# Float64 weights to two float32 words: low words added to 16 bits of the pattern in one operation, and two batches of k-v products moved to a later block

## The chip, the cores and the metric

The kernel runs on one core of a Trainium2 chip. The metric is the device time of one execution in microseconds, and the value before is the median of three runs. A profile is one further execution, taken by the hardware profiler.

## The reference, cut to what matters

```python
kv = np.einsum('bhsd,bhse->bhde', k, v)                # 8 batches, 8 heads, 576 tokens, 64 wide
out = np.einsum('bhsd,bhde->bhse', q, kv)
out = out / sqrt(mean(out * out, -1) + 1e-06) * g_norm
x = out as 4608 tokens x 512
h = x @ w_in                                           # w_in 512 x 2048, float64
x = (maximum(h, 0) ** 2) @ w_out                       # w_out 2048 x 512, float64
e = argmax(x @ w_gate + modality_bias[modality_id])    # 8 experts
out = softmax weight of e * (maximum(x @ w1[e], 0) @ w2[e])
```

w_in and w_out are float64 in memory. All products are made in float32 on TensorE, and each weight is split into a high and a low part of TensorE's own float32 format, so that one product of the reference is three products of the kernel (high by high, high by low, low by high).

## The kernel before, in words

The attention and the dense layer are one loop (phase 1) over 12 blocks of 2 to 4 token tiles of 128 tokens. A block j runs 16 iterations i. In each, `emit_h` makes one 128-wide slice of x @ w_in (12 matmuls into the tile `hps`), ScalarE and VectorE make the squared relu and split it (`relu`, `square`, `rest`, tile `ghl`), and `emit_x` adds the slice of two iterations earlier times w_out into the tiles `acc` (3 matmuls for each token tile). The attention of the next block's tiles runs between: `q_load`, `att_one`, `att_norm`, `att_tr`. Later blocks also compute the gate and split the expert weights w1 and w2 (`u_load`, `u_split`, `u_store`). After the 12 blocks follow the expert slots (phase 2).

Block 0 is different: it also turns the float64 weights into float32 parts. The weights are 32 pieces of 512 KB (16 of w_in, 16 of w_out, in the order in which they are used), and a piece is loaded raw into one of NRAW = 4 places of the tile `wq` (`w_load`). Every float64 is there as two 32-bit words, `low` and `up`. Iteration i of block 0 handles two pieces at each step: `w_sum`, `w_part` on pieces 2i + 4 and 2i + 5, `w_scale` and `w_join` on the next two. The steps are:

- `w_scale` (ScalarE): multiplies `up`, read as float32, by a power of two into the tile `conv` (L303). For three pieces of four it also turns `up` into a bare sign bit (L307, L308).
- `w_join` (VectorE): shifts the scaled pattern by three bits and sets the sign (L317 for two pieces at once, or L324, or L328 and L329 where the sign was not prepared).
- `w_sum` (VectorE): takes sign and exponent of the pattern (L339), multiplies the low word by it (L340), and adds that to the pattern as float32 (L342). As soon as L340 has read the low word, the place in `wq` is free and `w_load` of the piece four later is issued on the SP queue.
- `w_part`: ScalarE copies the high part (L356), and the low part is the difference (L354), on VectorE for w_in and on GpSimd (POOL) for w_out.

The order of every engine is the order in which the code is written; nothing reorders it. The SP queue issues nearly all loads in that order too, so a load that waits for its buffer holds up every load behind it.

The k-v products of a batch (`kv_load`, `kv_mm`) need 4 loads of 480 KB and 2 of 192 KB, and 4 groups of 20 small matmuls (tile `kvps`). Batch 0 comes ahead of block 0. Batches 1, 2 and 3 (FIRST = 4) are made in block 0, one group or two per iteration, into the tiles `early`. The products of batches 2 and 3 are stored in DRAM (`kvd`, L177) and fetched back by `kv_get` in a later block, because only two product tiles (`kvbd`) are kept. Batches 4 to 7 are made in blocks 5, 6, 8 and 9, two groups at iteration 2 and two at iteration 4, with loads into tiles of the pool `t4`.

Ahead of block 0 the SP queue loads weight pieces 0 to 3 between the k-v parts of batch 0 and the first four q tiles. VectorE converts four pieces before it turns to the sums of squares of the first tiles.

Of the kernel before, what the change touches and what calls it, by code (L numbers as in the profile page):

```python
# [10 lines left out]
F32 = mybir.dt.float32  # L11
# [3 lines left out]
U32 = mybir.dt.uint32  # L15
AF = mybir.ActivationFunctionType
# [23 lines left out]
NKV = 2  # L40

FIRST = 4
NRAW = 4
# [3 lines left out]
def body(ctx: ExitStack, tc: tile.TileContext, qT, kvp, kvr, g_norm, w_in, w_out, mod, wg, wgd, mb, w1, w2, out):  # L47
# [12 lines left out]
    kvd = dram.tile([FIRST, 128, 4, 64], F32, name="kvd")  # L60
# [68 lines left out]
    def kv_load(b, hp):  # L129
# [27 lines left out]
    def kv_mm(b, hp):  # L157
# [8 lines left out]
        if hp == 3:  # L166
            kvps.pop(b)
            if b < NKV or b >= FIRST:
                t = kvbd[b % NKV]
                lo, up = t[0:64, :, 0:64], t[64:128, :, 64:128]  # L170
            else:
                t = one.tile([128, 4, 64], F32, tag="x", name="kvs")
                lo, up = t[0:64], t[64:128]
            nc.scalar.activation(out=lo, in_=ps[0:64, :, 0:64], func=AF.Copy)
            nc.scalar.activation(out=up, in_=ps[64:128, :, 64:128], func=AF.Copy)
# [3 lines left out]
    def kv_get(b):
        t = kvbd[b % NKV]  # L180
        for h in range(2):
            c = slice(64 * h, 64 * h + 64)
            nc.sync.dma_start(out=t[c, :, c], in_=kvd[b, c])
# [106 lines left out]
    xb = p1b.tile([128, 512], U32, tag="sq", name="xb")  # L290
# [21 lines left out]
    def w_join(n, c=2):  # L312
        if n < NP:
            low, up, a = w_at(n, c)

            if n % 4 == 0 and c == 2:
# [3 lines left out]
                return  # L320
            for m in range(c):
                am, um = a[:, m], up[:, m]
                if (n + m) % 4 < 3:
                    nc.vector.scalar_tensor_tensor(  # L324
                        out=am, in0=am, scalar=3, in1=um, op0=ALU.logical_shift_left, op1=ALU.bitwise_or
                    )
                else:
                    nc.vector.tensor_scalar(out=am, in0=am, scalar1=3, scalar2=None, op0=ALU.logical_shift_left)  # L328
                    nc.vector.scalar_tensor_tensor(  # L329
# [846 lines left out]
```

## Time and profile before

| What | us |
|---|---|
| Median of three runs | 1466.36 (1461.36, 1466.36, 1468.72) |
| The profiled execution's own time | 1462.47 |
| Its span in the trace | 1460.7 |
| PE busy | 1405.7 (96%) |
| DVE busy | 794.5 (54%) |
| ACT busy | 534.9 (37%) |
| POOL busy | 451.3 (31%) |
| Chain that ended last | PE 81%, DVE 8%, DMA 4%, ACT 3% |

PE is TensorE, DVE VectorE, ACT ScalarE, POOL GpSimd, and SPq the queue of SyncE that issues loads. The busy shares are means over very different stages, and a busy PE is not PE at its peak, since its matmuls overlap. The trace can be cut into stretches: the preparation before the first matmul of block 0 (to 36.77 us), block 0 (to 162.78 us, where block 1's first matmul starts), the other blocks, and the expert slots from about 943 us on.

### The profile page before, as it was taken

How to read it: one execution, taken by the hardware profiler on the slowest of the kernel's cores; microseconds unless marked ns; L12 is line 12 of the kernel's file. 1: busy time of each engine (PE TensorE's matmuls, PEld its weight loads, DVE VectorE, ACT ScalarE, POOL GpSimd, SP SyncE). 2: the span in 40 equal slices, each digit the busy share in tenths (PEclk: the TensorE clock that was granted, in tenths of full speed). 3: DMA queues.
4: the chain of work that ended last, by engine and by line, in shares of the span. 5: the costliest groups of instructions: out<-in, count | busy, mean ns of one | idle time of the engine just before them, and what ended most of it. 6: DMA issues, size and time to landing. Idle time of an engine off the chain costs nothing.

```text
span 1460.7 us, 24807 instructions
## 1 busy us (share of the span) xinstructions
PE 1405.7 (96%) x7682; PEld 1211.8 (83%) x7682; DVE 794.5 (54%) x1618; ACT 534.9 (37%) x965; POOL 451.3 (31%) x392
## 2 busy tenths in 40 slices
PE   5698999999999999999999999999999999999997
PEld 4577798988998888988888988888888888888886
DVE  5798577868785658685858677262222222222221
ACT  5687434444333334433434433332222222222221
POOL 1123223635324434443434441222222222222210
PEclk9899999999999999999999999999999999999999
DMA  7974225665536565666566640644114623357762
GB/s 209 222 215 149 98 73 192 197 201 199 167 105 199 177 191 184 213 192 187 194 173 205 209 169 23 261 151 159 44 45 154 214 101 102 121 205 263 266 254 87
DMA packets 80817, 247.33 MB, mean 169 GB/s; under 512 B 15790, under 2 KB 16046, under 8 KB 72368
## 3 DMA queue, kind: packets, MB, share of 16 engines
q1 hardware_dynamic: 69552, 208.83, 44.1%
q0 software_dynamic: 8832, 20.09, 4.3%
q10 hardware_dynamic: 2304, 16.78, 2.9%
q8 instruction: 70, 1.15, 0.3%
q14 instruction: 59, 0.48, 0.1%
HBM read 414.59 MB, written 87.96 MB: 344 GB/s over the span
## 4 chain that ended last, share of the span: by engine, by line
PE 81%; DVE 8%; DMA 4%; ACT 3%; issue 2%; POOL 1%; SPq 0%; DVEq 0%; POOLq 0%; ACTq 0%
PE hps L395 22%; PE hps L901 15%; PE yps L938 15%; PE acc L445 7%; PE acc L443 7%; PE acc L444 7%; PE htp L926 2%; DMA wq<-w_in 2%; DVE ghl L430 1%; PE ops L211 1%; DVE r L429 1%; PE xps L881 1%; PE tps L267 1%; DVE xb L340 1%; DMA wq<-w_out 1%
## 5 line engine op out<-in xcount | busy, mean ns | idle before, releaser
L395 PE MATMUL hps<-xt,wa 128*128 128x384 f32 (+2 forms) x2304 | 441.0, 340 | 1.1 <-ACT xt L270 0.8
L395 PEld LDWEIGHTS hps<-xt,wa 128*128 128x128 f32 x2304 | 403.5, 189 | 24.3 <-ACT xt L270 1.2
L379 POOL TENSOR_TENSOR hl<-raw,hl 128x512 fp32r<-128x512 f32 x128 | 178.7, 1403 | 256.1 <-ACT hl L378 255.7
L938 PE MATMUL yps<-wb,hq 128*128 (+1 forms) x960 | 234.2, 399 | 0.4 <-ACT hq L927 0.4
L901 PE MATMUL hps<-wa,xq 128*128 (+1 forms) x960 | 233.7, 399 | 0.0
L443 PE MATMUL acc<-wb,ghl 128*128 128x512 f32 x576 | 231.0, 401 | 0.0
L445 PE MATMUL acc<-wb,ghl 128*128 128x512 f32 x576 | 227.4, 395 | 3.5 <-DVE ghl L430 3.5
L444 PE MATMUL acc<-wb,ghl 128*128 128x512 f32 x576 | 226.1, 393 | 0.0
L467 DVE SCALAR_TENSOR_TENSOR junk<-x,wg_sb 128x512 f32<-128x512 f32 x264 | 218.3, 827 | 4.8
L938 PEld LDWEIGHTS yps<-wb,hq 128*128 128x128 f32 x960 | 177.5, 188 | 41.2 <-ACT hq L927 0.7
L901 PEld LDWEIGHTS hps<-wa,xq 128*128 128x128 f32 x960 | 177.3, 188 | 39.6
L429 DVE TENSOR_TENSOR r<-r 128x384 f32<-128x384 f32 (+1 forms) x160 | 108.9, 681 | 177.4 <-ACT ghl L422 177.0
L412 ACT ACTIVATE r<-hps 128x384 f32<-128x384 f32 (+2 forms) x192 | 93.7, 488 | 295.8 <-PE hps L395 291.0
L430 DVE TENSOR_TENSOR ghl<-r,ghl 128x384 fp32r<-128x384 f32 (+2 forms) x192 | 138.5, 722 | 51.3 <-ACT r L424 33.1
L928 DVE TENSOR_TENSOR hq<-htp,hq 128x512 fp32r<-128x512 f32 x80 | 51.5, 686 | 206.2 <-ACT hq L927 206.2
L945 POOL DMA_INDIRECT out<-y,me x40 | 40.7, 1018 | 351.4 <-ACT y L944 287.5
L378 ACT ACTIVATE hl<-raw 128x512 fp32r<-128x512 f32 x128 | 80.2, 626 | 144.7 <-DMA raw<-w 101.3
L445 PEld LDWEIGHTS acc<-wb,ghl 128*128 128x128 f32 x576 | 108.0, 188 | 28.6 <-DVE ghl L430 4.8
L443 PEld LDWEIGHTS acc<-wb,ghl 128*128 128x128 f32 x576 | 108.4, 188 | 18.0 <-issue 0.5
L444 PEld LDWEIGHTS acc<-wb,ghl 128*128 128x128 f32 x576 | 108.4, 188 | 17.9
L422 ACT ACTIVATE ghl<-r 128x384 fp32r<-128x384 f32 (+2 forms) x192 | 100.9, 526 | 6.0
L944 ACT ACTIVATE y<-yps,me 128x512 f32<-128x512 f32 x40 | 27.5, 687 | 203.1 <-PE yps L938 192.3
(157 smaller groups left out, 1147.4 us busy)
## 6 DMA issues: line engine op xcount, KB each, us to landing
wa<-wd SPq DMA_DIRECT2D x148, 1024.0 KB
wb<-wd SPq DMA_DIRECT2D x144, 1024.0 KB
wd<-hl SPq DMA_DIRECT2D x128, 512.0 KB
raw<-w SPq DMA_DIRECT2D x128, 256.0 KB
x2buf<-x SPq DMA_DIRECT2D x36, 256.0 KB
wq<-w_in SPq DMA_DIRECT2D x16, 512.0 KB
wq<-w_out SPq DMA_DIRECT2D x16, 512.0 KB
qt<-qt SPq DMA_DIRECT2D x32, 256.0 KB
```

What stands on the lines that cost most here:

```text
L379: nc.gpsimd.tensor_tensor(out=hl[:, 1, :].bitcast(F32R), in0=t, in1=hl[:, 0, :], op=ALU.subtract)
L395: nc.tensor.matmul(ps[:, 0:128 * BLK[j]], wav[:, i, wi, k, :], xt[:, xi, k, :], start=(n == 0), stop=(n == 11))
L412: nc.scalar.activation(out=rs[i], in_=hps.pop(i)[:, 0:c], func=AF.Relu)
L422: nc.scalar.activation(out=g2[0], in_=r, func=AF.Square)
L429: nc.vector.tensor_tensor(out=r, in0=r, in1=r, op=ALU.mult)
L430: nc.vector.tensor_tensor(out=g2[1], in0=r, in1=g2[0].bitcast(F32), op=ALU.subtract)
L443: nc.tensor.matmul(a, g2[0][:, sl], wbv[:, i, 0, :], start=(i == 0), stop=False)
L444: nc.tensor.matmul(a, g2[0][:, sl], wbv[:, i, 1, :], start=False, stop=False)
L445: nc.tensor.matmul(a, g2[1][:, sl], wbv[:, i, 0, :], start=False, stop=(i == NF - 1))
L467: nc.vector.scalar_tensor_tensor(out=junk, in0=x2s[j, t], scalar=1.0, in1=wg_sb[:, e, :], op0=ALU.mult, op1=ALU.mult, accum_out=lgs[j][:, ...
L901: nc.tensor.matmul(hp[f], xq[:, xi, k, :], rhs(wa, s, o + 512 * wi), start=(k == 0 and n == 0), stop=(k == 3 and n == 2),)
L938: nc.tensor.matmul(ps, hq[:, hi, k, :], rhs(wb, s, 1024 * k + 512 * wi), start=(k == 0 and n == 0), stop=(k == 7 and n == 2),)
```

## The change

The change has four parts.

1. `w_sum` becomes one VectorE operation for two pieces: the low word times 2**-29 is added to the low 16 bits of the joined pattern (a 16-bit view of every second halfword), and the sum is rounded to 16-bit integers. L339, L340, L342 and the tile `xb` go. Both loads of the pieces four later are issued behind that one operation.
2. `w_scale` prepares the sign bit for one piece of four only, and `w_join` therefore uses the two-operation form for three pieces of four. The low parts of w_out are subtracted on VectorE, not on GpSimd.
3. The products of batches 2 and 3 move from block 0 to blocks 1 and 3, in the form that batches 4 to 7 have. The store and fetch through `kvd` go. The q tiles of block 1's attention are loaded at iterations 4, 7 and 10 of block 0, before at 6, 8 and 10. The units of the expert weights have fewer places in blocks 2 and 3, and the last of them move to blocks 10 and 11.
4. Ahead of block 0 the k-v parts of batch 0 are loaded first, then q tiles and weight pieces in turn. Only pieces 0 and 1 are converted before the attention of the first tiles is through; pieces 2 to 5 follow behind it.

```diff
-FIRST = 4
 NRAW = 4
...
-        if b < FIRST:
+        if b < NKV:
             t = early[-1][0:120, n % 3 if b else hp]
...
-            if NKV <= b < FIRST:
-                nc.sync.dma_start(out=kvd[b], in_=t)
...
-            k = sum(m % 4 < 3 for m in range(n, n + c))
-            if k:
-                up = up[:, 0:k]
+            if n % 4 == 0:
+                up = up[:, 0]
...
     def w_join(n, c=2):
+        for n in range(n, min(n + c, NP)):
+            low, up, a = (t[:, 0] for t in w_at(n, 1))
+            if n % 4 == 0:
                 nc.vector.scalar_tensor_tensor(
                     out=a, in0=a, scalar=3, in1=up, op0=ALU.logical_shift_left, op1=ALU.bitwise_or
                 )
+            else:
+                nc.vector.tensor_scalar(out=a, in0=a, scalar1=3, scalar2=None, op0=ALU.logical_shift_left)
+                nc.vector.scalar_tensor_tensor(
+                    out=a, in0=up, scalar=0x80000000, in1=a, op0=ALU.bitwise_and, op1=ALU.bitwise_or
+                )
...
     def w_sum(n, c=2):
-        for n in range(n, min(n + c, NP)):
-            low, up, a = w_at(n, 1)
-            low, a = low[:, 0], a[:, 0]
-            x = xb.bitcast(F32)
-            nc.vector.tensor_scalar(out=xb, in0=a, scalar1=0xFF800000, scalar2=None, op0=ALU.bitwise_and)
-            nc.vector.scalar_tensor_tensor(out=x, in0=low, scalar=2.0**-52, in1=x, op0=ALU.mult, op1=ALU.mult)
-            w_load(n + NRAW)
-            nc.vector.tensor_tensor(out=a.bitcast(F32), in0=a.bitcast(F32), in1=x, op=ALU.add)
+        if n < NP:
+            low, up, a = w_at(n, c)
+            h = a.bitcast(U16).rearrange("p m (f c) -> p m f c", c=2)[:, :, :, 0]
+            nc.vector.scalar_tensor_tensor(out=h, in0=low, scalar=2.0**-29, in1=h, op0=ALU.mult, op1=ALU.add)
+            for m in range(c):
+                w_load(n + m + NRAW)
...
-                eng = nc.gpsimd if m else nc.vector
-                eng.tensor_tensor(out=p[1], in0=w, in1=p[0].bitcast(F32), op=ALU.subtract)
+                nc.vector.tensor_tensor(out=p[1], in0=w, in1=p[0].bitcast(F32), op=ALU.subtract)
...
+    for hp in range(4):
+        kv_load(0, hp)
+    q_load(0)
     w_load(0)
-    kv_load(0, 0)
+    q_load(1)
+    q_load(2)
     w_load(1)
-    kv_load(0, 1)
-    kv_load(0, 2)
+    q_load(3)
     w_load(2)
-    kv_load(0, 3)
-    q_load(0)
-    q_load(1)
     w_load(3)
-    q_load(2)
-    q_load(3)
...
+    w_part(1, True, 1)
+    w_join(2)
+    w_sum(2)
+    w_scale(4)
+    w_part(2, False)
     w_join(4)
+    w_part(2, True)
...
-            if b < FIRST:
-                i = max(n // 2, n - 2)
+            if b < NKV:
+                i = n // 2
...
-                i0 = 2 * n + 6 if j == 0 else 3 * n + 3
+                i0 = 3 * n + (4 if j == 0 else 3)
...
-            for b in kv_gt.get((j, i), []):
-                kv_get(b)
```

How the change moves instructions, at three places. The first is VectorE in the middle of block 0, one iteration of the program before, from one `rest` (L430) to the next. `conv` is the joined pattern, `wq` the raw words, `xb` the factor for the low word.

```order
L430 TENSOR_TENSOR ghl<-r,ghl 128x512
L324 SCALAR_TENSOR_TENSOR conv<-conv,wq 128x512
L328 TENSOR_SCALAR conv<-conv 128x512
L329 SCALAR_TENSOR_TENSOR conv<-wq,conv 128x512
L354 TENSOR_TENSOR wa<-conv,wa 128x512
L339 TENSOR_SCALAR xb<-conv 128x512
L340 SCALAR_TENSOR_TENSOR xb<-wq,xb 128x512
L342 TENSOR_TENSOR conv<-conv,xb 128x512
L339 TENSOR_SCALAR xb<-conv 128x512
L340 SCALAR_TENSOR_TENSOR xb<-wq,xb 128x512
L342 TENSOR_TENSOR conv<-conv,xb 128x512
```

The same iteration on VectorE in the changed program, where L403 is `rest`, L300, L304 and L305 are `w_join`, L327 is the low part and L314 is the new sum.

```order
L403 TENSOR_TENSOR ghl<-r,ghl 128x512
L300 SCALAR_TENSOR_TENSOR conv<-conv,wq 128x512
L304 TENSOR_SCALAR conv<-conv 128x512
L305 SCALAR_TENSOR_TENSOR conv<-wq,conv 128x512
L327 TENSOR_TENSOR wb<-conv,wb 128x512
L327 TENSOR_TENSOR wa<-conv,wa 128x512
L314 SCALAR_TENSOR_TENSOR conv<-wq,conv 128x1024
```

Six operations of the sums have become one of twice the width, and the low part of w_out has come over from GpSimd. In every other iteration the join has two L304 and two L305.

The SP queue in block 0, before: the loads of four weight pieces (L287), and behind each pair parts of a later batch (L140, L149).

```order
L287 DMA wq<-w_out 128x1024
L287 DMA wq<-w_in 128x1024
L140 DMA early<-kvp 120x1024
L149 DMA rem<-kvr 96x512
L287 DMA wq<-w_out 128x1024
L287 DMA wq<-w_in 128x1024
L140 DMA early<-kvp 120x1024
L287 DMA wq<-w_out 128x1024
```

The SP queue there in the changed program, from the loads behind batch 1 on (L604 is the initial state of a table, L272 a weight piece, L177 a q tile).

```order
L604 DMA tab<-ini 2176x1x68
L272 DMA wq<-w_out 128x1024
L272 DMA wq<-w_in 128x1024
L272 DMA wq<-w_out 128x1024
L272 DMA wq<-w_in 128x1024
L272 DMA wq<-w_out 128x1024
L272 DMA wq<-w_in 128x1024
L177 DMA qt<-qt 128x512
L272 DMA wq<-w_out 128x1024
L272 DMA wq<-w_in 128x1024
```

The parts of batches 2 and 3 have left this stretch of the queue; only weight pieces and three q tiles are left behind the table.

## Rows read from the trace of the kernel before

**Rows 1.** The page's chain of work that ended last, by engine
```profile
PE 81%; DVE 8%; DMA 4%; ACT 3%; issue 2%; POOL 1%; SPq 0%; DVEq 0%; POOLq 0%; ACTq 0%
```

**Rows 2.** By stretch: us, busy of PE, PEld, DVE, ACT, POOL; PE clock; DMA share; GB/s
```profile
53.08:157.23 104.15, 90.46 (x559) 71.80 (x557) 91.18 (x128) 72.85 (x105) 28.55 (x20) 0.95 0.67 189
...
172.48:900.00 727.52, 719.13 (x4104) 646.70 (x4103) 523.19 (x1115) 286.11 (x558) 287.02 (x216) 1.00 0.55 175
```

**Rows 3.** Timeline of PE in block 0: start, us, engine, line, operation, tiles, shapes
```profile
53.08 4.84 PE L395 MATMUL hps<-xt,wa 128*128 128x512 f32 x12
...
79.32 3.02 PE L395 MATMUL hps<-xt,wa 128*128 128x512 f32 x12
82.18 0.39 PE L443 MATMUL acc<-wb,ghl 128*128 128x512 f32 x1
...
84.99 0.69 PE L155 MATMUL kvps<-early 120*64 120x64 f32 x16
...
85.72 3.02 PE L395 MATMUL hps<-xt,wa 128*128 128x512 f32 x12
...
157.23 2.99 PE L395 MATMUL hps<-xt,wa 128*128 128x512 f32 x12
```

**Rows 4.** Waits of PE, 53 to 158 us: total, times, longest
```profile
PE kvps L155 <- DMA early<-kvp: 6.6, 3, 3.0
```

**Rows 5.** DVE groups by shape, 37 to 160 us: count, busy us, mean ns, idle before
```profile
L342 DVE TENSOR_TENSOR conv<-conv,xb 128x512 f32<-128x512 f32 x28 | 23.2, 829 | 1.0
L340 DVE SCALAR_TENSOR_TENSOR xb<-wq,xb 128x512 f32<-128x512 uint32 x28 | 19.4, 693 | 1.0
L354 DVE TENSOR_TENSOR wa<-conv,wa 128x512 fp32r<-128x512 f32 x13 | 15.5, 1189 | 0.0
L339 DVE TENSOR_SCALAR xb<-conv 128x512 uint32<-128x512 uint32 x28 | 11.8, 422 | 0.5
...
L317 DVE SCALAR_TENSOR_TENSOR conv<-conv,wq 128x1024 uint32<-128x1024 uint32 x7 | 8.6, 1222 | 7.3 <-ACT wq L308 6.0 <-issue 1.3
```

**Rows 6.** ACT groups by shape, 37 to 160 us: the scaling of the weights
```profile
L303 ACT ACTIVATE conv<-wq 128x1024 f32<-128x1024 f32 x13 | 14.8, 1142 | 12.5 <-DMA wq<-w_in 11.7 <-DVE wa L354 0.8
...
L307 ACT ACTIVATE wq<-wq,tiny 128x512 f32<-128x512 f32 x7 | 5.5, 779 | 0.2
L308 ACT ACTIVATE wq<-wq 128x512 int32<-128x512 f32 x7 | 4.8, 680 | 0.2
```

**Rows 7.** Timelines of SPq and ACT in block 0: weight loads and their first users
```profile
54.95 4.34 SPq L287 DMA_DIRECT2D wq<-w_out  x1
...
68.23 1.12 ACT L303 ACTIVATE conv<-wq 128x1024 f32<-128x1024 f32 x1 [3.51 <-DMA wq<-w_in]
...
83.55 0.35 SPq L287 DMA_DIRECT2D wq<-w_out  x1
85.43 0.35 SPq L287 DMA_DIRECT2D wq<-w_in  x1
...
91.34 1.14 ACT L303 ACTIVATE conv<-wq 128x1024 f32<-128x1024 f32 x1 [1.92 <-DMA wq<-w_in]
```

**Rows 8.** Timeline around 72 us: a low part on POOL and one on DVE
```profile
72.34 1.87 POOL L354 TENSOR_TENSOR wb<-conv,wb 128x512 fp32r<-128x512 f32 x1 [12.46 <-ACT wb L356]
...
72.98 1.78 DVE L354 TENSOR_TENSOR wa<-conv,wa 128x512 fp32r<-128x512 f32 x1
```

**Rows 9.** Timelines ahead of iteration 2: PE's last group of batch 0; SPq's first of batch 1
```profile
19.77 1.33 PE L155 MATMUL kvps<-early 120*64 120x64 f32 x20 [3.17 <-DMA early<-kvp]
...
42.14 0.44 SPq L140 DMA_DIRECT2D early<-kvp  x1
```

**Rows 10.** Timeline of PE in block 5, where batch 4 is made
```profile
436.29 2.25 PE L395 MATMUL hps<-xt,wa 128*128 128x384 f32 x12
...
441.95 2.27 PE L395 MATMUL hps<-xt,wa 128*128 128x384 f32 x12
...
446.14 2.27 PE L395 MATMUL hps<-xt,wa 128*128 128x384 f32 x12
```

More of the change, by code (lines that the diff above doesn't have):

```diff
@@ L15 @@
 U32 = mybir.dt.uint32
+U16 = mybir.dt.uint16
 AF = mybir.ActivationFunctionType
@@ L59, in body @@
     tab = dram.tile([PAD + 128, 4], I32, name="tab")
-    kvd = dram.tile([FIRST, 128, 4, 64], F32, name="kvd")
     wd = dram.tile([E, NPIECE, 128, 2, 2, 512], F32, name="wd")
@@ L144, in kv_load @@
                 t = early[0][0:96, hp // 2, :].rearrange("p (a b c) -> p a b c", a=2, b=2)
-            elif b < FIRST:
+            elif b < NKV:
                 t = g_p.tile([96, 2, 2, 128], F32, tag="ghl", name="rem")
@@ L167, in kv_mm @@
             kvps.pop(b)
[L168 to L175, printed above, removed]
-            if NKV <= b < FIRST:
-                nc.sync.dma_start(out=kvd[b], in_=t)
[L179 to L183, printed above, removed]
+            t = kvbd[b % NKV]
+            nc.scalar.activation(out=t[0:64, :, 0:64], in_=ps[0:64, :, 0:64], func=AF.Copy)
+            nc.scalar.activation(out=t[64:128, :, 64:128], in_=ps[64:128, :, 64:128], func=AF.Copy)
     q_t = {}
@@ L289, in body @@
     conv = [t4_p.tile([128, 2, 512], U32, tag="t4", name="conv") for _ in range(2)]
-    xb = p1b.tile([128, 512], U32, tag="sq", name="xb")
     tiny = const.tile([128, 1], F32, name="tiny")
@@ L312, in w_join @@
     def w_join(n, c=2):
-        if n < NP:
-            low, up, a = w_at(n, c)
-            if n % 4 == 0 and c == 2:
+        for n in range(n, min(n + c, NP)):
+            low, up, a = (t[:, 0] for t in w_at(n, 1))
+            if n % 4 == 0:
                 nc.vector.scalar_tensor_tensor(
@@ L319, in w_join, with w_sum @@
                 )
[L320 to L342 removed]
+            else:
[3 more added lines that the diff above has]
+                )
+    def w_sum(n, c=2):
+        if n < NP:
+            low, up, a = w_at(n, c)
+            h = a.bitcast(U16).rearrange("p m (f c) -> p m f c", c=2)[:, :, :, 0]
+            nc.vector.scalar_tensor_tensor(out=h, in0=low, scalar=2.0**-29, in1=h, op0=ALU.mult, op1=ALU.add)
+            for m in range(c):
+                w_load(n + m + NRAW)
     def w_part(n, lo, c=2):
@@ L596, in body @@
     warm(10)
-    w_part(2, False, 1)
-    w_scale(3, 1)
-    w_part(2, True, 1)
-    w_join(3, 1)
-    w_sum(3, 1)
+    w_scale(0, 1)
+    w_join(0, 1)
+    w_sum(0, 1)
     n0 = BLK[0]
@@ L607, in body @@
         sqs.append(att_sq(T))
+        if T == 0:
+            w_part(0, False, 1)
         if T == 1:
-            w_part(3, False, 1)
+            w_scale(1, 1)
     for T in range(n0):
         att_sum(sqs[T], ss[:, 8 * T:8 * T + 8])
+        if T == 0:
+            w_part(0, True, 1)
         if T == 1:
-            w_part(3, True, 1)
+            w_join(1, 1)
+            w_sum(1, 1)
     warm(50)
@@ L620, in body @@
     ms = att_rms(ss, n0, True)
-    w_scale(4)
+    w_part(1, False, 1)
+    w_scale(2)
     ri = att_inv(*ms)
@@ L948, in st_d @@
         )
-    kv_ld, kv_pr, kv_gt = {}, {}, {}
+    kv_ld, kv_pr = {}, {}
     for b in range(1, 8):
@@ L963, in body @@
                 kv_pr.setdefault((j, 2 * (hp // 2) + 2), []).append((b, hp))
-        if NKV <= b < FIRST:
-            kv_gt.setdefault((BLOCK[b * 576 // 128] - 1, 2), []).append(b)
     kv_blocks = {j for j, i in kv_ld}
```

16 lines of the change are left out of this document (removed).

## The prediction

> **What bounds the kernel now.** I read the chain of waits first: PE holds 81% of it, DVE 8% and DMA 4% [rows 1]. Then I cut the span into stretches. From 172.48 to 900 us PE is busy 719.13 of 727.52 us, so whatever is added to PE there is paid in full. In block 0, between the start of iteration 2 (53.08 us) and that of iteration 15 (157.23 us), PE is busy for 90.46 of 104.15 us only, and DVE for 91.18 [rows 2]. These 13 iterations have a pitch of 104.15 / 13 = 8.01 us. The timeline of PE shows what an iteration needs when nothing waits: 2.86 us for emit_h, 2.81 for emit_x and 0.73 for a group of k-v products, 6.40 in all from 79.32 to 85.72 us [rows 3]. So block 0 loses about 1.6 us an iteration, and the PE waits by name are few: 6.6 us for k-v parts [rows 4]. The rest is PE at the lower of its two clock levels (mean granted clock 0.95 in this stretch), and the loads of the k-v parts are late because they stand in the SP queue behind weight loads that wait for DVE's L340. What sets the pace is therefore the conversion of the weights: DVE, and the way of a place in wq round its loop.
>
> **Part 1, the steps of the conversion.** Prices are means from [rows 5] and [rows 6]. Before, DVE spends on a piece's sum 0.42 (L339) + 0.69 (L340) + 0.83 (L342) = 1.94 us, on two pieces 3.88. The new sum is one operation on 1024 elements. No row has a 16-bit operand of this size. The nearest row is L317, also two operands and two steps on 1024 elements, 1.22 us. I bound it below by 0.61 (half of that, if 16-bit elements went at twice the rate) and above by 2.44 (if each halfword cost two passes). I take 1.22, since the shape and the form are L317's.
>
> Over two iterations, that is four pieces, DVE then has: two sums 2.44; joins 0.69 for the piece with a prepared sign and 3 x (0.42 + 0.69) for the others, 4.02 (priced like L340 and L339); four low parts and two rests, plain two-operand steps on 512 elements like L340, 4.14; 10.6 in all or 5.3 an iteration. Three attention tiles with three such steps each add 6.2 us, 0.5 an iteration: 5.8. Before, the same account gives 7.76 for the sums, 1.22 + 0.69 + 0.42 + 0.69 = 3.02 for the joins, 2.38 for two low parts of w_in (1.19 each) and 1.38 for the rests, 14.5 or 7.3 an iteration, plus the same 0.5. (The busy time of [rows 2] is lower, since the last sums stand in iteration 13.) L354's 1.19 holds a collision: while POOL makes its own low part, 1.87 us at 72.34, DVE's takes 1.78 us [rows 8]. With POOL's part gone, this goes too. ACT was busy for 72.85 of the 104.15 us [rows 2] and loses the signs of two pieces in four. So neither DVE nor ACT is full any more at a pitch over 5.8.
>
> **The loop of a place in wq** is next. There are four places, so a sum must be followed by load, scale, join and the next sum of the same place within two iterations. After the change both loads start when the common sum ends. How long a load pair then takes is the disputed term. In the trace, ACT waited for such a pair at 91.34 us: 5.9 us from the second issue (85.43), 7.8 from the first (83.55) [rows 7]. Now both are issued together and less other traffic runs, so the pair lies between these bounds, 5.0 (allowing for the k-v part behind it there) and 7.8; I take 6.3. The loop that holds the piece with a prepared sign is the longer one: sum 1.22 + load 6.3 + scale 1.14 + 0.78 + 0.68 + join 0.69 + 0.42 + 0.69 + low parts 1.38 = 13.3 us, or 6.65 an iteration. That is more than PE's own need: 2.86 + 2.81 without k-v products, and with one pair of k-v groups and three attention tiles, each priced like two groups, 13 x 5.67 + 8 x 0.73 = 79.6 us or 6.1 an iteration. So I expect a pitch of 6.65, and 13 x (8.01 - 6.65) = **17.7 us saved** between iterations 2 and 15. After that the tail is PE's and unchanged.
>
> The Trainium skill, "DMA: Bandwidth & Descriptors", section "Anatomy of one DMA — SWDGE (gpsimd) path", fits a DMA that GpSimd issues as about 2.0 us plus its bytes over 436 GB/s. For 1 MB in a pair that would be an estimate of 4.4 us, below every wait of [rows 7]; the loop would fall to 5.7 an iteration and PE's 6.1 would rule.
>
> **Part 2, the start.** Batch 0's last group starts at 19.77 us, behind three weight pieces in the queue [rows 9]. With 1.5 MB less ahead of it, at block 0's 189 GB/s [rows 2], it comes up to 8 us earlier; the last q tile gains less, but DVE converts two pieces less before the last sums of squares. I put the first matmul of block 0 about 7 us earlier. But DVE then has, behind the attention, one low part, two joins and a sum, two more joins, two low parts and a sum: 0.69 + 2.22 + 1.22 + 1.80 + 1.38 + 1.22 = 8.5 us until the sum that frees the queue for batch 1's parts, against 1.22 + 1.94 + 0.42 + 0.69 = 4.3 before. Those parts were issued at 42.14 us [rows 9] and move to about 39, so iteration 2, which waits for them, comes **3 us earlier**, between 0 and 7. The gain of 7 is nearly all given to this wait: that is what is late next.
>
> **Part 3, the moved products.** In block 5 an iteration with two groups of k-v products lasts 441.95 - 436.29 = 5.66 us, the next one without 446.14 - 441.95 = 4.19 [rows 10]; 1.47 us a pair. Four pairs, in blocks 1 and 3, cost 5.9 us where PE has no slack. PE's stops in the later blocks are 727.52 - 719.13 = 8.4 us [rows 2], under 1 us a block; for two fuller blocks I add 1.1: **7 us added** in all, between 5.9 and 9. Their removal from block 0 is already in the new pitch. The loads in block 1 stand behind the gate's weights (2 MB) in the SP queue. Both are issued when the conversion ends, more than two iterations of block 0 and two of block 1 before PE needs the products, some 20 us for 3.2 MB; at 189 GB/s that takes 17 us, so I cost it at nothing. If the cover were gone, PE would wait a few us once. The store and fetch of kvd go at no cost; three units of expert weights that move to blocks 10 and 11 are hidden there by PE.
>
> **The sum:** -17.7 - 3 + 7 = -13.7 us. The profiled execution took 1462.47 us, which gives 1448.8. The median of the three runs is 3.9 us above that execution, so against the median the forecast is **1453 us**. About 0.5%, 7.3 us, is what a measurement of this kernel can tell from no change.
>
> **The rivals.**
>
> *A, PE rules block 0.* If a pair of loads lands in 5.0 us, the loop is 12.0 or 6.0 an iteration and falls below PE's 6.1 (a sum of 0.61 alone leaves it at 6.35): 13 x (8.01 - 6.1) = 24.8, so -24.8 - 3 + 7 = -20.8 and 1445.6 us. For it speaks that the parts of two batches, 4.7 MB, are no longer fetched beside the weights; against it, that in no row of the trace did a pair land so soon. Chance 0.18. The DMA page's estimate above would bring this case about; by that rule the gain would be half as large again, and the trace does not agree with it so far.
>
> *B, the loop hardly gets shorter.* At 7.8 us for a pair, the loop is 14.8 or 7.4 an iteration: -7.9 - 3 + 7 = -3.9, 1462.5 us. A 16-bit sum of 2.44 us gives nearly the same: 7.26 an iteration and 1460.6. For it speaks that the two loads no longer start 1.9 us apart, so that the first gains no lead. Chance 0.20.
>
> *C, slower.* Both loads issued at once queue up in the DMA engines. The issue at 54.95 us shows what that does: it took 4.34 us by itself, and the user started 13.3 us later at 68.23 [rows 7]. At 8.4 us a pair the whole change comes out at zero; from 9.5 on it is slower by over 0.5%; at 10 the pitch is 8.5, so 6.4 is lost, and with -3 + 7 the time is 1477. Against it: that row had k-v parts and the table's many small pieces in the queue, which the later iterations don't have. Chance 0.07.
>
> The forecast's own case has 0.55. The range reaches from A's middle over B to its end: 1442 to 1464; C and the far part of A are left out. The chance of faster by over 0.5% (below 1459, a pitch under 7.14) is 0.72: the forecast's case nearly whole, with A. Within 0.5%: 0.20. Slower: 0.08.
>
> **What would show it.** The first matmul of iteration 15 should start near 137 us, block 1's first near 142 (162.78 before), and pitches in block 0 should lie near 6.6 us, with ACT's L287 waiting for DMA as the longest stop in every other iteration. The new sum should read 1.2 us. The low parts on DVE should read 0.69 without the long ones. PE waits for batches 2 and 3 should be absent in blocks 1 and 3, whose iterations 2 and 4 should be 1.5 us longer. I am wrong if DVE is busy over 9 us in 10 all through block 0 (the sum is dearer), if a pair of loads takes over 8 us, or if PE waits in block 1 for k-v parts behind the gate's weights.

## The result and the profile after

The changed kernel takes **1452.51 us** (median of five runs, 1451.13 to 1453.27), against 1468.72 us for the kernel before on the same chip (five runs, 1461.36 to 1470.1). The ratio is 0.9899, with a 95% interval of 0.9874 to 0.9925: faster by about 1%. The forecast of 1453 us holds, and so does its sign. In a later comparison (e9 below) the changed kernel took 1454.98 us and the ratio was 0.991. So medians of different comparisons may stand 2 to 3 us apart, and what follows leans on ratios and on the traces.

The two profiled executions lie nearer together: 1453.12 us now, 1462.47 before, a difference of 9.35. The execution that was profiled before lies 6.3 us below the median of its kernel, the one profiled now 0.6 above its own. Since the sum of the prediction was made against that execution, it is checked against these 9.35 us. Where an execution at the median before spends its 6 us more is in no trace.

In the changed program L368 is emit_h, L416 to L418 are emit_x, L153 the k-v products, L252 the transposes of an attention tile, L272 a weight load, L287 the scaling on ScalarE, L290 and L291 the prepared sign, L300, L304 and L305 the join, L314 the new sum, L327 a low part, L403 `rest`. First the page's line of busy times.

```profile
PE 1405.7 (97%) x7682; PEld 1213.2 (84%) x7682; DVE 765.4 (53%) x1578; ACT 513.8 (35%) x946; POOL 430.5 (30%) x376
```

PE's busy time is the same as before to a tenth of a microsecond. What has gone is idle time of PE, in block 0.

The same stretches as in [rows 2], by the same columns: the first four lines cut block 0 from iteration 2 (53.19) to iteration 15 (138.36), the fifth is all of it, the last runs from block 1's first matmul to the experts' first transposes.

```profile
53.19:62.22 9.03, 9.03 (x66) 7.16 (x65) 5.90 (x9) 2.18 (x3) 0.00 (x0) 0.76 1.13 204
62.22:90.80 28.58, 28.58 (x140) 23.42 (x137) 18.51 (x29) 21.91 (x34) 0.00 (x0) 1.00 0.59 188
90.80:109.32 18.52, 14.87 (x62) 12.03 (x60) 14.19 (x22) 13.01 (x20) 3.19 (x2) 0.82 0.44 155
109.32:138.36 29.04, 29.04 (x140) 24.21 (x138) 24.40 (x38) 20.22 (x32) 8.25 (x4) 1.00 0.47 179
53.19:138.36 85.17, 81.52 (x399) 66.82 (x397) 63.00 (x96) 57.32 (x88) 11.44 (x6) 0.93 0.57 180
143.91:933.81 789.90, 779.12 (x4530) 699.10 (x4529) 548.58 (x1184) 306.00 (x599) 296.49 (x225) 1.00 0.54 176
```

The stretch of that last line in the trace before:

```profile
162.78:943.49 780.71, 772.32 (x4370) 694.30 (x4369) 542.79 (x1184) 305.67 (x595) 295.64 (x226) 1.00 0.53 172
```

The 13 iterations take 85.17 us, where they took 104.15 [rows 2]. DVE's busy time in them fell from 91.18 to 63.00. In three of the four pieces PE never stops (28.58 of 28.58 us, 29.04 of 29.04); all of the 3.65 us that PE stands still lies between 90.80 and 109.32, and there (0.82) and in iteration 2 (0.76) the granted clock is below 1. In the later blocks PE's busy time rose from 772.32 to 779.12 us, which is what the moved products cost it, and its idle time from 8.4 to 10.8.

PE's timeline in block 0 and the next block (start, duration, engine, line, operation, tiles, shapes, count, and the wait before it):

```profile
53.19 5.03 PE L368 MATMUL hps<-xt,wa 128*128 128x512 f32 x12
...
90.80 2.88 PE L368 MATMUL hps<-xt,wa 128*128 128x512 f32 x12
...
100.05 1.12 PE L252 MATMUL tps<-ident,x 128*128 128x128 f32 x4 [3.65 <-DVE x L239]
100.82 5.09 PE L368 MATMUL hps<-xt,wa 128*128 128x512 f32 x12
...
109.32 2.98 PE L368 MATMUL hps<-xt,wa 128*128 128x512 f32 x12
...
138.36 3.00 PE L368 MATMUL hps<-xt,wa 128*128 128x512 f32 x12
...
143.91 2.27 PE L368 MATMUL hps<-xt,wa 128*128 128x384 f32 x12
...
153.65 2.27 PE L368 MATMUL hps<-xt,wa 128*128 128x384 f32 x12
159.34 2.27 PE L368 MATMUL hps<-xt,wa 128*128 128x384 f32 x12
163.53 2.27 PE L368 MATMUL hps<-xt,wa 128*128 128x384 f32 x12
169.21 2.27 PE L368 MATMUL hps<-xt,wa 128*128 128x384 f32 x12
```

Iteration 15 starts at 138.36 (157.23 before, [rows 3]) and block 1 at 143.91 (162.78 before): 18.9 us earlier. The rows at 90.80, 100.82 and 109.32 are iterations 8, 9 and 10: these two steps take 10.02 and 8.50 us, against 5.44 to 6.6 in the other iterations from 3 on. PE waits 3.65 us for one attention tile, and the emit_h behind that wait takes 5.09 us for a work that takes 2.88 to 3.02 in the other iterations from 3 on, part of it at the lower clock level of 1.2 GHz (the granted clock is 0.50 from 100.05 to 104.00 us). In block 1, iterations 2 and 4 last 159.34 - 153.65 = 5.69 and 169.21 - 163.53 = 5.68 us, which are 1.5 us more than the 4.19 between them.

DVE's groups from 37 to 160 us, the columns those of [rows 5]:

```profile
L314 DVE SCALAR_TENSOR_TENSOR conv<-wq,conv 128x1024 uint16<-128x1024 uint32 x15 | 20.3, 1354 | 0.0
L305 DVE SCALAR_TENSOR_TENSOR conv<-wq,conv 128x512 uint32<-128x512 uint32 x21 | 14.5, 692 | 0.7
...
L327 DVE TENSOR_TENSOR wb<-conv,wb 128x512 fp32r<-128x512 f32 x16 | 10.9, 685 | 0.1
L327 DVE TENSOR_TENSOR wa<-conv,wa 128x512 fp32r<-128x512 f32 x14 | 9.6, 684 | 0.0
L304 DVE TENSOR_SCALAR conv<-conv 128x512 uint32<-128x512 uint32 x21 | 8.9, 426 | 3.7 <-ACT conv L287 3.7
```

The new sum takes 1.35 us for two pieces, where the three operations took 3.88. The low parts are at 0.68, and the long ones of [rows 5] (mean 1.19) are gone. The last two views of the changed kernel are the SP queue and its user on ScalarE: first the table's write and the pair behind it, then an undisturbed pair.

```profile
50.56 0.60 SPq L604 DMA_DIRECT2D tab<-ini  x1
53.96 6.17 SPq L272 DMA_DIRECT2D wq<-w_out  x1
60.18 0.42 SPq L272 DMA_DIRECT2D wq<-w_in  x1
...
75.28 0.33 SPq L272 DMA_DIRECT2D wq<-w_out  x1
75.70 0.38 SPq L272 DMA_DIRECT2D wq<-w_in  x1
```

```profile
68.30 1.12 ACT L287 ACTIVATE conv<-wq 128x1024 f32<-128x1024 f32 x1 [3.26 <-DMA wq<-w_in]
...
80.16 1.13 ACT L287 ACTIVATE conv<-wq 128x1024 f32<-128x1024 f32 x1 [1.95 <-DMA wq<-w_in]
...
93.81 1.12 ACT L287 ACTIVATE conv<-wq 128x1024 f32<-128x1024 f32 x1 [3.26 <-DMA wq<-w_in]
```

The undisturbed pair is in use 80.16 - 75.28 = 4.9 us after the first issue. The pair behind the table's write stands 6.17 us in issue, and its user comes 14.3 us after that issue began.

### The profile page after: what moved, and what is told of

Same layout as the page of the kernel before. It is cut to its first block, busy times and chain, and to the rows that moved or that the text cites. A ratio compares the mean times of both kernels' runs of the same rounds, so it can differ in the third digit from the quotient of the medians.

```text
span 1451.4 us, 24693 instructions
## 1 busy us (share of the span) xinstructions
PE 1405.7 (97%) x7682; PEld 1213.2 (84%) x7682; DVE 765.4 (53%) x1578; ACT 513.8 (35%) x946; POOL 430.5 (30%) x376
## 5 line engine op out<-in xcount | busy, mean ns | idle before, releaser
L368 PE MATMUL hps<-xt,wa 128*128 128x384 f32 (+2 forms) x2304 | 442.8, 341 | 0.8 <-ACT xt L255 0.8
L368 PEld LDWEIGHTS hps<-xt,wa 128*128 128x128 f32 x2304 | 405.5, 190 | 24.4 <-ACT xt L255 1.2
L416 PE MATMUL acc<-wb,ghl 128*128 128x512 f32 x576 | 231.5, 402 | 0.0
L440 DVE SCALAR_TENSOR_TENSOR junk<-x,wg_sb 128x512 f32<-128x512 f32 x264 | 224.6, 851 | 4.8
L418 PE MATMUL acc<-wb,ghl 128*128 128x512 f32 x576 | 227.0, 394 | 0.0
L385 ACT ACTIVATE r<-hps 128x384 f32<-128x384 f32 (+2 forms) x192 | 93.6, 488 | 305.1 <-PE hps L368 297.6
L403 DVE TENSOR_TENSOR ghl<-r,ghl 128x384 fp32r<-128x384 f32 (+2 forms) x192 | 139.8, 728 | 51.5 <-ACT r L397 33.5
L418 PEld LDWEIGHTS acc<-wb,ghl 128*128 128x128 f32 x576 | 108.1, 188 | 23.9
L416 PEld LDWEIGHTS acc<-wb,ghl 128*128 128x128 f32 x576 | 108.4, 188 | 18.4 <-issue 0.5
L885 DVE TENSOR_SCALAR hr<-hps 128x512 f32<-128x512 f32 x36 | 24.9, 692 | 141.1 <-PE hps L869 141.1
```

Of the source, the lines that this page charges most:

```text
L368: nc.tensor.matmul(ps[:, 0:128 * BLK[j]], wav[:, i, wi, k, :], xt[:, xi, k, :], start=(n == 0), stop=(n == 11))
L385: nc.scalar.activation(out=rs[i], in_=hps.pop(i)[:, 0:c], func=AF.Relu)
L403: nc.vector.tensor_tensor(out=g2[1], in0=r, in1=g2[0].bitcast(F32), op=ALU.subtract)
L416: nc.tensor.matmul(a, g2[0][:, sl], wbv[:, i, 0, :], start=(i == 0), stop=False)
L418: nc.tensor.matmul(a, g2[1][:, sl], wbv[:, i, 0, :], start=False, stop=(i == NF - 1))
L440: nc.vector.scalar_tensor_tensor(out=junk, in0=x2s[j, t], scalar=1.0, in1=wg_sb[:, e, :], op0=ALU.mult, op1=ALU.mult, accum_out=lgs[j][:, ...
```

## The experiments

Each experiment is an edit of the changed kernel, except e3, which is one of the kernel before, and e9, which is the changed kernel once more. Times are medians; the ratio is to the kernel before on the same chip, with its 95% interval. The starts are from each run's own timeline of PE, in us.

| Run | Time | Ratio (interval) | Iteration 2 | Iteration 15 | Block 1 | Experts' first transposes |
|---|---|---|---|---|---|---|
| before | 1468.72 | 1 | 53.08 | 157.23 | 162.78 | 943.49 |
| changed | 1452.51 | 0.9899 (0.9874 to 0.9925) | 53.19 | 138.36 | 143.91 | 933.81 |
| e1 old sum | 1477.97 | 1.0078 (1.0052 to 1.0104) | 60.10 | 160.71 | 166.23 | 955.23 |
| e2 products back in block 0 | 1459.27 | 0.9945 (0.9928 to 0.9963) | 53.49 | 150.26 | 155.82 | 938.82 |
| e3 before, products moved | 1471.0 | 1.0022 (1.0009 to 1.0036) | 52.86 | 155.15 | 161.10 | 951.89 |
| e4 low parts on GpSimd | 1459.24 | 0.994 (0.9921 to 0.9959) | 54.88 | 140.76 | 146.33 | 938.89 |
| e5 no prepared sign | 1449.57 | 0.9874 (0.9844 to 0.9904) | 53.05 | 132.92 | 138.47 | 930.16 |
| e6 loads delayed | 1465.1 | 0.9977 (0.9962 to 0.9992) | 54.98 | 144.51 | 150.08 | 940.94 |
| e7 old start | 1459.15 | 0.9934 (0.991 to 0.9957) | 58.59 | 143.29 | 148.85 | 938.30 |
| e8 batch 1 early | 1450.88 | 0.9886 (0.9857 to 0.9914) | 43.99 | 132.70 | 138.27 | 928.39 |
| e9 changed, again | 1454.98 | 0.991 (0.9895 to 0.9926) | 54.36 | 139.79 | 145.35 | 935.39 |
| e10 table early | 1447.26 | 0.9858 (0.9838 to 0.9878) | 52.68 | 132.16 | 137.72 | 928.56 |
| e11 e8 and e5 | 1445.37 | 0.9845 (0.9827 to 0.9863) | 45.23 | 130.52 | 136.08 | 926.26 |
| e12 e8, e5 and e10 | 1450.33 | 0.9878 (0.9858 to 0.9898) | 48.63 | 133.71 | 139.27 | 929.76 |

### e1: the old sum back

```diff
-            h = a.bitcast(U16).rearrange("p m (f c) -> p m f c", c=2)[:, :, :, 0]
-            nc.vector.scalar_tensor_tensor(out=h, in0=low, scalar=2.0**-29, in1=h, op0=ALU.mult, op1=ALU.add)
...
+            nc.vector.tensor_scalar(out=xb, in0=a, scalar1=0xFF800000, scalar2=None, op0=ALU.bitwise_and)
+            nc.vector.scalar_tensor_tensor(out=x, in0=low, scalar=2.0**-52, in1=x, op0=ALU.mult, op1=ALU.mult)
+            w_load(n + NRAW)
+            nc.vector.tensor_tensor(out=a.bitcast(F32), in0=a.bitcast(F32), in1=x, op=ALU.add)
```

> The changed kernel with the three operations per piece of the sum put back (all else of the change stays). Theory one, the conversion of the weights (VectorE and the way of a place round load, scale, join, sum) sets the pace of block 0: VectorE has again 7.8 us of sums in two iterations where the change has 2.7, its need rises to about 8.3 us an iteration, the pitch from 6.55 to about 8.3, and the time by 13 x 1.75 = 23 us to about 1475. Rival, the moved k-v loads and PE made the gain: the time stays within 5 us of the changed kernel's 1452.5.

It took 1477.97 us, 25.5 more than the changed kernel and slower than the kernel before. The 13 iterations take 160.71 - 60.10 = 100.61 us, 7.74 each, and iteration 2 itself comes 6.9 us later, because the k-v parts of batch 1 stand behind longer sums. PE's waits from 0 to 180 us (total, times, longest):

```profile
PE kvps L153 <- DMA early<-kvp: 22.6, 6, 13.9
PE acc L421 <- DVE ghl L406: 13.1, 7, 2.5
```

The second line is not there in the changed kernel: VectorE makes `ghl` only after its sums. In the trace, 15.4 us of the difference lie in the 13 iterations and 6.9 ahead of them. The pitch is below the 8.3 that was expected, yet the rival's 5 us are far exceeded: the conversion sets the pace when the sum is dear, as the prediction read it.

### e2 and e3: the place of the products alone, with the new conversion and with the old

```diff
-            if b < NKV:
-                i = n // 2
+            if b < FIRST:
+                i = max(n // 2, n - 2)
...
-                i0 = 3 * n + (4 if j == 0 else 3)
+                i0 = 2 * n + 6 if j == 0 else 3 * n + 3
```

That is e2, with the store and fetch of the two product tiles and FIRST = 4 back as well. e3 is the kernel before with FIRST = 2 and the same two lines in the other direction.

> The changed kernel with the products of batches 2 and 3, their store and fetch and the q loads back in block 0. Theory one: blocks 1 to 11 lose the 9.2 us that the moved products cost there, and block 0 gains 8 groups of 0.73 us on PE, their loads in front of the weight loads and one wait on the store, 8 to 12 us: 1450 to 1456, no difference to speak of. Rival: the place of the products decides; block 0 goes back to a pitch near 8 and the time to over 1460.

> The kernel before with nothing but the products of batches 2 and 3 moved to blocks 1 and 3 (and the q loads as in the change). Theory one: VectorE's 7.8 us an iteration stay, block 0 gains at most 13 x 0.2 = 3 us and one wait of 4 us, the blocks pay 9 us: 1468 to 1474 against 1468.7. Rival, the k-v loads held up block 0: 10 us or more gained there, the time at or below 1465.

Putting the products back costs 6.8 us (1459.27; 5.0 between the traces), more than expected for e2, though its pitch, 7.44, is not the rival's 8 either. Moving them in the kernel before costs 2.6 us by the medians (1471.0 against 1468.39 in the same comparison), as expected. Between the traces it is 8.4 (951.89 against 943.49), because the profiled execution before lies so far below its median. The traces say why the two parts depend on one another. With the old conversion the 13 iterations take 155.15 - 52.86 = 102.29 us without the products and took 104.15 with them: VectorE sets the pace, and PE's products fit beside it. With the new conversion they take 150.26 - 53.49 = 96.77 us with the products and 85.17 without. There PE's own work counts: of the 11.6 us, 8.0 are busy time of PE (89.54 against 81.52). The rest is waits, 7.2 us against 3.65; 6.4 of the 7.2 are for the parts, whose loads share the queue with the weights. From block 1's first matmul to the experts' first transposes it is 780.7 us before, 783.0 in e2, 789.9 in the changed kernel and 790.8 in e3: the products cost 6.9 to 10.1 us there.

### e4: low parts of w_out back on GpSimd

```diff
-                nc.vector.tensor_tensor(out=p[1], in0=w, in1=p[0].bitcast(F32), op=ALU.subtract)
+                eng = nc.gpsimd if m else nc.vector
+                eng.tensor_tensor(out=p[1], in0=w, in1=p[0].bitcast(F32), op=ALU.subtract)
```

> The changed kernel with the low parts of w_out back on GpSimd. Theory one: VectorE loses one 0.69 us step per iteration, but its own low part beside it lasts about 1.8 instead of 0.69 us, so the loop of a place gets some 0.4 us longer in each round or 0.2 us an iteration: 1453 to 1457. Rival, VectorE's load is what counts: 0.69 us less in an iteration, 1444 to 1449.

It took 1459.24 us, 6.7 more, and more than expected. VectorE loses 16 low parts of 0.68 and yet gains nothing (DVE's groups from 37 to 150 us, then GpSimd's, then one step of each engine from the timeline):

```profile
L305 DVE SCALAR_TENSOR_TENSOR conv<-wq,conv 128x512 uint32<-128x512 uint32 x21 | 19.4, 923 | 0.7
L304 DVE TENSOR_SCALAR conv<-conv 128x512 uint32<-128x512 uint32 x21 | 17.6, 840 | 4.1 <-ACT conv L287 4.1
```

```profile
L328 POOL TENSOR_TENSOR wb<-conv,wb 128x512 fp32r<-128x512 f32 x16 | 22.3, 1396 | 70.6 <-ACT wb L330 70.6
```

```profile
72.75 1.33 POOL L328 TENSOR_TENSOR wb<-conv,wb 128x512 fp32r<-128x512 f32 x1 [12.03 <-ACT wb L330]
72.85 1.52 DVE L304 TENSOR_SCALAR conv<-conv 128x512 uint32<-128x512 uint32 x1
```

On average the 21 L304 take 0.84 instead of 0.43 us, and the 21 L305 0.92 instead of 0.69: 21 x (0.41 + 0.23) = 13.4 us, more than the 16 x 0.68 = 10.9 that went. It is the collision of [rows 8] once more, not on the low part, as was expected, but on the join. The averages hide how it goes: 13 steps take 1.5 to 1.67 us, the others 0.41 to 0.46 and 0.69 as in the changed kernel. Each of the 13 begins while GpSimd's low part runs and ends 0.3 us (L304) or 0.55 us (L305) after it, as in the two lines above (74.08 and 74.37). The low part of [rows 8] ends 0.55 us after GpSimd's as well (74.76 and 74.21). Yet the pitch from iteration 2 to 15 is only 0.05 us longer (6.61). Of the 5.1 us that the trace shows, 1.7 lie ahead of iteration 2, 0.7 in the 13 iterations and 2.7 in the later blocks; what the last are wasn't settled.

### e5 and e6: a shorter and a longer round of a place in wq

```diff
-            if n % 4 == 0:
-                up = up[:, 0]
-                nc.scalar.activation(out=up.bitcast(F32), in_=up.bitcast(F32), func=AF.Sign, bias=tiny)
-                nc.scalar.activation(
-                    out=up.bitcast(I32), in_=up.bitcast(F32), func=AF.Copy, scale=2.0**30, bias=-2.0**30
-                )
...
```

That is e5, with all joins made in two steps. e6 writes over the raw low words behind their sum, which the next loads of that place must wait for:

```diff
+            if n >= 4:
+                nc.gpsimd.memset(low, 0)
             for m in range(c):
                 w_load(n + m + NRAW)
```

> The changed kernel without the two ScalarE steps that prepare a sign for one piece in four; that piece is joined by the two VectorE steps that the others already have. In the round of a place of wq this takes out 0.78 + 0.68 of ScalarE and adds 0.43 of VectorE, about 1.0 us in two iterations. Theory L (the round of a place paces block 0): 0.5 us less per iteration, up to 6 us in all, 1446 to 1449. Theory P (PE's own need paces most iterations, and the rest are single stops): under 2 us of change, 1450.5 to 1454.

> The changed kernel with a GpSimd write of zeros over the raw low words behind each sum, for which the next loads of these places must wait. It lengthens only the round of a place (by the time of one such write, 1 to 2 us in two iterations) and takes nothing on PE, VectorE or ScalarE; the values are overwritten by the load. Theory L: 0.5 to 1 us more per iteration, 6 to 13 us in all, 1459 to 1465. Theory P: at most 3 us, up to 1456.

e5 took 1449.57 us. Its median is 3 us lower, at the edge of what these comparisons tell apart, but block 1 starts 5.4 us earlier. Its pitch is (132.92 - 53.05) / 13 = 6.14 us against 6.55. e6 took 1465.1 us, with a pitch of 6.89, and block 1 starts 6.2 us later. The write in e6 took this long:

```profile
L316 POOL MEMSET wq<- 128x1024 uint32 x14 | 14.7, 1049 | 77.0 <-DVE conv L314 77.0
```

(The medians differ by more, 12.6 us; e6's ten runs lie from 1460.1 to 1467.9, and the profiled one is the lowest.) So 1.0 us off a round and 1.05 us on it moved the pitch by -0.41 and +0.34 us, out of 0.5 either way. By size that is theory L's. By place it is not: 4.7 of the 5.4 us that e5 gains are in iterations 8 and 9, which take 7.50 and 6.36 us there, against 10.02 and 8.50. And 3.7 of the 4.4 us that e6 loses in its 13 iterations are in iterations 11 to 14 (117.27 to 144.51, against 114.85 to 138.36). Nor is e6 as clean an edit as was expected: twice its write stands behind GpSimd's steps for an attention tile, so that the loads follow their sum 3.4 us later (116.94 + 1.33 to 121.65) instead of 1.1, and three L304 beside a write take 0.9 us instead of 0.42. Both runs thus show that the round has little slack, not that it paces every iteration. The round, at 12.4 us (sums at 99.92 and 112.31) to 12.7 (112.31 and 125.01), and PE's own need in two iterations are nearly equal, so that neither has any slack to make up for a delay. That leaves the question where the delay of iteration 8 comes from, which e10 answers.

### e7 and e8: the start

e7 puts the first loads back into the order of before. e8 issues three of batch 1's four parts ahead of block 0:

```diff
         att_tr(T, *((ps_acc, "acc") if T < 2 else (ps_att, "att")))
+    for hp in range(3):
+        kv_load(1, hp)
     w_part(1, True, 1)
...
-                kv_ld.setdefault((0, i), []).append((b, hp))
+                if hp == 3:
+                    kv_ld.setdefault((0, i), []).append((b, hp))
```

> The changed kernel with the first loads in the order of the kernel before (weight pieces between the parts of batch 0 and the q tiles). Theory W (iteration 2 waits for the k-v parts of batch 1, whose loads are let go by VectorE's first two pair sums, so the earlier first matmul is given back there): the first matmul of block 0 is 3 to 5 us later, iteration 2 starts within 2 us of 53.2, and the end is within 3 us of 1452.5. Rival (the new order is worth what the first matmul shows): 4 us slower, 1456 to 1457.

> The changed kernel with three of the four parts of batch 1 (k and v) loaded ahead of block 0, not at its iteration 0. Theory W: PE's wait of 8.5 us ahead of iteration 2 goes; what comes next there is the third pair of weight pieces, so iteration 2 comes 3 to 7 us earlier and the end 2 to 7 us earlier, 1446 to 1450. Rival (iteration 2 is held by the weights as much as by batch 1): within 1.5 us of 1452.5.

My theory for e7 fell. The time is 1459.15 us, 6.6 more, and PE's timeline shows that the old order is paid in full at iteration 2:

```profile
37.14 8.04 PE L368 MATMUL hps<-xt,wa 128*128 128x512 f32 x24 [0.78 <-ACT xt L255]
54.12 1.12 PE L153 MATMUL kvps<-early 120*64 120x64 f32 x16 [8.93 <-DMA early<-kvp]
```

The first matmul is 4.7 us later and iteration 2 5.4 (58.59). The wait for batch 1 is 8.9 us long in e7 and 8.5 in the changed kernel; it doesn't shrink by what the first matmul loses. Both ends of it hang on the same VectorE: the sums that let go the queue come behind the attention's last step, whenever that is (batch 1's first load is issued at 46.95 in e7, 4.7 us later as well). The new order of loads thus is worth 5.4 us at iteration 2. With the old order and the rest of the change, iteration 2 starts 5.5 us later than before (58.59 against 53.08). That this is the new train of conversions alone is read from the program, since e7 holds the other parts too.

e8 takes that wait away, and iteration 2 starts at 43.99, 9.2 us earlier. Of this, 5.7 us are left at iteration 15 and 5.4 at the experts' first transposes. The medians show 1.6 us (1450.88), within the uncertainty of the two; e11 against e5 shows 3.9 us in the trace and 4.2 in the medians (of two comparisons) for the same edit. So it is worth some 4 us, not the 9 that the wait shows: PE comes sooner to weights that are not there sooner. In e8, PE waits 5.1 us ahead of iteration 2 for ScalarE's relu (L385), which stands behind a scaling (41.29) that waited 3.95 us for its weights.

### e9 to e12: the table's write, and the best version

```diff
     warm(50)
+    tab_init()
...
-                if i == 2:
-                    tab_init()
```

> The changed kernel once more, as the yardstick for the three beside it, which differ from it by a few us. Expected: within 2 us of 1452.5.

> The changed kernel with the table's initial state written ahead of block 0, not in its iteration 2, where the next weight load stood 6.17 us in issue behind that write. Theory T (this stall delays the weights of iterations 4 and 5, and the round of a place carries the delay on): the pair that landed at 68.3 us lands 2 to 5 us earlier and the end comes 1 to 4 us earlier. Rival (PE has other work until those weights are used, or the write's many small pieces now delay the first loads): within 1 us of the yardstick, or slower.

The changed kernel came out 2.5 us above its first median (e9), where 2 were expected. That one edit (e10) brought 7.7 us against e9, nearly twice the most that theory T gave: 1447.26 us. Three views of e10: ScalarE's user of the pair that had stood behind the table, PE at the starts of iterations 8, 9 and 10, and the stretch from iteration 2 to 15.

```profile
64.77 1.12 ACT L287 ACTIVATE conv<-wq 128x1024 f32<-128x1024 f32 x1
```

```profile
90.61 2.88 PE L368 MATMUL hps<-xt,wa 128*128 128x512 f32 x12
96.41 2.99 PE L368 MATMUL hps<-xt,wa 128*128 128x512 f32 x12
102.77 2.98 PE L368 MATMUL hps<-xt,wa 128*128 128x512 f32 x12
```

```profile
52.68:132.16 79.48, 79.38 (x398) 65.10 (x397) 62.85 (x96) 57.36 (x88) 11.72 (x6) 0.97 0.52 175
```

The pair is in use at 64.77 instead of 68.30 and ScalarE does not wait for it. Iterations 8 and 9 take 5.80 and 6.36 us, 6.4 less than in the changed kernel, which is more than the whole difference of the 13 iterations (85.17 - 79.48 = 5.7). PE is now busy for 79.38 of 79.48 us: its own work is the bound, to a tenth. That the write's place costs this stop is shown by the run, and the other runs agree: with the write in iteration 2, PE waits for the same attention tile in e4 to e9 and e11 too (0.5 to 3.9 us), and with the early write not in e10 nor e12. The steps between are read from the two traces. A write of many small pieces at 50.56 holds the next weight load 6.17 us in issue. From there the conversions run 3.3 to 3.5 us later than in e10 (sums at 73.81, 79.02, 85.68 and 91.48 against 70.31, 75.52, 82.42 and 88.23), and the round has no slack to make it good. Some thirty microseconds on, an attention tile, whose steps stand behind the conversion on VectorE, is late by 4.8 us (its step L239 starts at 99.31 against 94.47), and PE waits 3.65 us for it (100.05 in the changed kernel). Then the granted clock is 0.50 until 104 us, which costs 0.5 us in the transposes and 2.1 in iteration 9.

One piece stays open, the 1.5 us between those 3.3 and the 4.8. In the changed kernel the pair issued at 87.13 is in use only at 93.81, 6.7 us later, though its last packets moved by 91.5. It is no accident of one execution: the same pair takes 6.3 to 6.5 us in e4, e5, e7, e8, e9 and e11, but 5.4 in e6 and 5.0 in e10. An instruction fetch stands in the trace at 91.7, but which engine it was for isn't shown, and no run was made on it.

> The changed kernel with three parts of batch 1 loaded ahead of block 0 and without the prepared signs. If the two gains stand at different places (the start of block 0 for the one, the pitch for the other), they add up in the trace: block 1 starts about 5 + 5 = 10 us earlier than in the changed kernel, near 134, and the time is 6 to 10 us below the yardstick. If the earlier start only brings PE sooner to the weights, little is added to the 5 us of the one alone: 3 to 5 us below.

> Early batch 1, no prepared signs and the early table together: the version that should beat both kernels. By theory T 1 to 4 us below the run without the early table; by its rival the same as that run or slower.

e11, batch 1 early and no prepared sign, is the best of all: 1445.37 us, 9.6 below e9 and 1.5% below the kernel before. Block 1 starts at 136.08. The gains add up in part: 7.8 us there against the changed kernel, or 9.3 against e9, where e5 and e8 alone have 5.4 and 5.6. e12, with the table early as well, is 5 us worse than e11. What was early for the table is late for the weights: ScalarE's first scaling in block 0, and PE's iteration 2, in e12:

```profile
45.95 1.11 ACT L287 ACTIVATE conv<-wq 128x1024 f32<-128x1024 f32 x1 [8.44 <-DMA wq<-w_in]
```

```profile
48.63 4.98 PE L357 MATMUL hps<-xt,wa 128*128 128x512 f32 x12 [7.92 <-ACT r L374]
```

Here the table's pieces and batch 1's parts stand in the queue ahead of the weight pair issued at 36.32, which is in use 9.6 us later. With only one of the two ahead of it, it is 5.0 us (e11) or 5.2 (e10). ScalarE waits 8.4 us for it (3.9 in e11), iteration 2 starts 3.4 us after that of e11, and the end is as much later (929.76 against 926.26). The early table without batch 1's parts (e10 and e5 together) wasn't tried.

## Why the prediction was right, and where it was not

| Step | Predicted | Measured in the trace |
|---|---|---|
| 13 iterations of block 0 | -17.7 | 85.17 - 104.15 = -19.0 |
| Iteration 2 | -3 | 53.19 - 53.08 = +0.1 |
| Later blocks | +7 | 789.9 - 780.7 = +9.2 |
| Sum | -13.7 | -9.7 (experts at 933.81 against 943.49) |

**The reading holds in the main.** The conversion set the pace before (e1 puts it back, and the time goes up by 25.5 us; e3 takes the products out, and block 0 hardly gets shorter), and its shortening is what the change brings. One line of it was incomplete: [rows 4] shows one of four waits. The others, for the same stretch of the kernel before:

```profile
PE acc L445 <- DVE ghl L430: 3.5, 2, 3.0
PE ops L211 <- ACT kvs L175: 2.3, 1, 2.3
PE tps L267 <- DVE x L254: 1.4, 1, 1.4
```

With the 6.6 us for k-v parts they are all of the 13.7 us that PE stood idle there, and 4.9 of them are waits for VectorE by name, so "the rest" is not only the clock.

The pitch of 6.55 us lies by the forecast's 6.65, the low parts read 0.68, ScalarE's L287 waits for its load pair in every other iteration (1.4 to 3.3 us), no PE wait for batches 2 and 3 shows in blocks 1 and 3, and their iterations 2 and 4 are 1.5 us longer.

**The sum of both pieces** was taken at 1.22 us and is 1.35, well inside its bounds.

**The load pair was mis-sized**: "I take 6.3" turned out 4.9 to 5.0 us where nothing else is in the queue (75.28 to 80.16; 101.31 to 106.17; 113.76 to 118.78), 5.0 to 5.1 in e10, and 6.7 only for the pair left open above. That is the condition of rival A, and A's mechanism is what the iterations show: 28.58 and 29.04 us at a stretch without a stop of PE. In e10 all 13 take 79.48 us, where PE's need was worked out as 79.6; that is 24.7 less than before, where rival A had 24.8. The match is closer than it deserves, since 2.4 of the 79.48 us are iteration 2 at the lower clock (its emit_h takes 5.38 us, the others 2.88 to 3.02). The Trainium skill, "DMA: Bandwidth & Descriptors", section "Anatomy of one DMA — SWDGE (gpsimd) path", whose fit for a DMA that GpSimd issues gave an estimate of 4.4 us for the pair, was nearer than my choice; the trace has 4.9.

**So the pitch was right by luck, through two errors.** PE's need was the pace, 79.48 / 13 = 6.11 us (e10), and one stop in iterations 8 and 9, which costs 5.7 us in all, or 0.44 for each of the 13, raised it to 6.55. The prediction had seen its cause, since it named the 4.34 us issue behind the table's write [rows 7], but used it only for rival C, as something that "the later iterations don't have". They don't, but they inherit it.

**Iteration 2** is the step that failed outright: "comes 3 us earlier". The first matmul moved by 4.3 us (32.43 against 36.77), not 7: batch 0's last group, for which up to 8 us were allowed, starts at 15.69 against 19.77, 4.1 earlier. And the train of conversions ahead of batch 1's parts took 9.2 us (33.07 to the issue at 42.25), not 8.5. The issue is where it was, at 42.25 against 42.14 [rows 9].

**The later blocks** gave back 9.2 instead of 7: PE's idle time rose from 8.4 to 10.8 us, 2.4 more where 1.1 was allowed, all of it in waits for attention tiles (18 where there were 14), and its busy time rose by 6.8 us, where four pairs were priced at 5.9. Where the 0.9 lies isn't settled.

The sum thus was 4 us too good for the profiled executions (-13.7 against -9.7). That the median was met to half a microsecond is luck: the profiled execution before lies 6.3 us below its median and the one now 0.6 above, so that the medians differ by 16.2 us.

## What to carry to other kernels

When the stage that sets the pace is made cheaper, work out the need of every other stage to the same tenth: here the round of a buffer and PE's own work came out nearly equal, and then a single late transfer is no longer absorbed but arrives some thirty microseconds later at another engine, where the lower clock behind the wait adds to it. Look for such one-time delays (a write in small pieces in front of the loads) as soon as the steady state has no slack. Two parts of a change are not a sum of two prices: moving the products cost 2.6 us with the old conversion and brought 6.8 with the new one.

## What was not expected of the hardware

- A strided 16-bit operation on 1024 elements, with one 32-bit and one 16-bit operand, takes 1.35 us; the like operation on 32-bit words (L317 in [rows 5]) takes 1.22. Half-width elements were no faster here.
- A VectorE step of the join that begins while GpSimd subtracts a low part does not end before it (e4): the one-operand L304 then takes 1.5 us instead of 0.42 and ends 0.3 us after GpSimd's, the two-operand L305 takes 1.66 instead of 0.69 and ends 0.55 after. This holds for all 13 steps of the join that began so.
- The write of the table, 2176 rows, holds the next issue on the same queue for 6.17 us, 2.71 in e8 and 4.34 before, while its own issue reads 0.60. In e10, where the next issue comes 11 us after the write's, it reads 0.33.
